# Loading the filter rows of a spectral layer: GpSimd gathers against strided loads on the SP queue

## The chip, the core and the metric

The kernel runs on one core of a Trainium2 chip. The metric is device microseconds from the start to the end of one execution. A profile of one execution shows the five engines of the core: TensorE (PE, with its weight loads shown as PEld), VectorE (DVE), ScalarE (ACT), GpSimd (POOL) and SyncE (SP). SP computes nothing here. It issues DMAs, which run on 16 DMA engines that all issuers share. The row labelled SPq, ACTq or POOLq is the issue of a DMA, not its data movement.

## What is computed

The inputs are `x` (1 x 2048 x 640), a complex filter `w_r + i w_i` (2048 x 321), and the three weights of a gated feed-forward layer (640 x 1536 twice, 1536 x 640), all in bf16.

```python
def reference(A_x, A_w_r, A_w_i, B_x, B_w_gate, B_w_up, B_w_down):
    def _A_ref(x, w_r, w_i):
        X = rfft2(x)                    # over rows and columns: 2048 x 321, complex
        X = X * (w_r + 1j * w_i)
        return irfft2(X, s=(S, D))
    def _B_ref(x, w_gate, w_up, w_down):
        return (_gelu(x @ w_gate) * (x @ w_up)) @ w_down
    x = A_x
    xn = _layernorm(x, axis=-1)
    s = _A_ref(xn, A_w_r, A_w_i)
    g = _silu(_B_ref(xn, B_w_gate, B_w_up, B_w_down))
    return x + s * g
```

So there are two branches on the same normalised `xn`: a two-dimensional Fourier filter, and a feed-forward layer with 2048 x 640 x 1536 multiply-adds three times over. They meet only in the last line.

## The kernel before

The feed-forward branch is plain matmul work: `gate_up` (L806, matmuls on L818, gelu on ACT at L830, product on DVE at L834) and `down` (L846, matmuls on L878, then tanh on ACT at L887 and DVE at L892), in four groups of 512 rows. PE fills its time with it whenever the spectral branch has nothing ready.

The spectral branch has three stages.

* **Forward, first half.** `stats`, `apply` and `fold` normalise `x` and fold it. Two matmuls (L497, L498) per slab do the first part of the row transform, and the result goes to a DRAM scratch `D2` in eight stores. The task of store `j` is called `stored[j]`. Other slabs are transposed for the feed-forward branch by DMA (`turn_dma`, L461).
* **`spectral(G)`, for G = 0 to 7.** Four DMAs (`regroup`, L533) read `D2` back into `BU` in another order. For each block G of 128 frequency pairs, PE transforms (`sp<-T,BU` on L601 and, for two of the blocks, L584), ACT or DVE copies the result out of PSUM (`Z`, `zt`), PE transforms along the row (L624, L631), and DVE multiplies by the filter: `m1` on L663 and `m3` on L671, both `mc<-WF,mb`, read the filter tile `WF`. PE then transforms back (L706), ACT or DVE copies to `IU`, and SP stores it to a scratch `D3`.
* **Inverse, second half.** Four DMAs bring `D3` back, and `inverse` (L728) runs from about 152 us on.

A frequency k and its mirror S - k are worked on together, so each block needs two sets of 128 filter rows, of `w_r` and of `w_i` each. Row numbers of a block are not contiguous: a lane's row is `8 G + c + 128 k1`, with c from 0 to 7 and k1 from 0 to 15, and its mirror is 2048 minus that. `make_tables` (L29) writes the row numbers into a table `LANE`, and `gather(G)` (L548) issues four indirect DMAs on POOL (L557), of 128 rows of 642 bytes each, into `WF[G % 3]`. There are three such tiles, so the gather for block G waits until `m3` of block G - 3 has read its tile. Before the gathers of blocks 1 and 2 stands a one-element copy on POOL (`gate`, L554), which reads `BU` and so holds these gathers back until part of `BU` has landed.

Block 0 is special: rows 0 and 1024 and the rows 64 + 128 j stand in one block, in lanes that don't follow the formula.

The order on every engine is worked out beforehand by a planner (`Plan`, L127). Each piece of work is a task with an engine, an occupation and a latency in ns, a rank, and the tasks it comes after. A DMA's landing is modelled by one shared wire (`self.wire`, L199) that is pushed back by each DMA's size. The planner's result is only an order: each engine runs its instructions in that order. What an instruction really waits for on the chip are the data it reads and the buffers it overwrites, not the planned time and not the `after` list. The gather is planned with 4200 ns on POOL; a DMA issue on SP or ACT with 430 ns.

Of the kernel before, what the change touches and what calls it, by code (L numbers as in the profile page):

```python
# [28 lines left out]
def make_tables():  # L29

    th = 2 * np.pi / D
    n2 = np.arange(128)
    n1 = np.arange(16)
    f1 = np.zeros((128, 128))
    for g in range(NG):
        for s in range(4):
            k2 = 4 * g + s
            f1[:, 8 * g + s] = np.cos(2 * np.pi * n2 * k2 / 128)
            f1[:, 8 * g + 4 + s] = -np.sin(2 * np.pi * n2 * k2 / 128)
    f1[:, 4] = np.cos(np.pi * n2)  # L40
    t2 = np.zeros((NG, 2, 4, 16, 2, 16, 4))
    ti = np.zeros((NG, 2, 16, 4, 2, 4, 16))
    for g in range(NG):
        for s in range(4):
            k2 = 4 * g + s
            for k1 in range(16):
                if k2 == 0 and k1 == 0:
                    t2[g, 0, s, :, 0, 0, s] = 1
                    t2[g, 0, s, :, 1, 0, s] = (-1.0) ** n1
                    ti[g, 0, 0, s, 0, s, :] = 1  # L50
                    ti[g, 1, 0, s, 0, s, :] = (-1.0) ** n1
                elif k2 == 0:
                    part = 0 if k1 < 8 else 1
                    ph = 2 * np.pi * n1 * (128 * k1 if k1 < 8 else 64 + 128 * (k1 - 8)) / S
                    t2[g, part, s, :, 0, k1, s] = np.cos(ph)
                    t2[g, part, s, :, 1, k1, s] = -np.sin(ph)
                    ti[g, 0, k1, s, part, s, :] = np.cos(ph)
                    ti[g, 1, k1, s, part, s, :] = -np.sin(ph)
                else:
                    ph = 2 * np.pi * n1 * (k2 + 128 * k1) / S  # L60
                    c, sn = np.cos(ph), np.sin(ph)
                    t2[g, 0, s, :, 0, k1, s] = c
                    t2[g, 1, s, :, 0, k1, s] = sn
                    t2[g, 0, s, :, 1, k1, s] = -sn
                    t2[g, 1, s, :, 1, k1, s] = c
                    ti[g, 0, k1, s, 0, s, :] = c
                    ti[g, 1, k1, s, 0, s, :] = -sn
                    ti[g, 0, k1, s, 1, s, :] = sn
                    ti[g, 1, k1, s, 1, s, :] = c
    t2 = t2.reshape(NG, 128, 128).transpose(1, 0, 2)  # L70
    ti = ti.reshape(NG, 128, 128).transpose(1, 0, 2)
    d = np.arange(160) + 0.5
    je = np.arange(0, 321, 2)
    jo = np.arange(1, 322, 2)
    ce = np.cos(th * np.outer(d, je))
    ce[:, 160] = 0
    co = np.cos(th * np.outer(d, jo))
    co[:, 160] = 0
    se = np.sin(th * np.outer(d, je))
    se[:, 0] = 0  # L80
    so = np.sin(th * np.outer(d, jo))
    so[:, 160] = 0
    fm = np.stack([ce, co, se, so, -ce, -co])[:, 0:128].transpose(1, 0, 2)
    ft = np.concatenate([ce[128:], so[128:], co[128:], se[128:]])
    ft = np.stack([ft, -ft], axis=1)
    nn = 0.5 / (S * D)
    wc = np.full(161, 2 * nn)
    wc[0] = nn
    wc[160] = 0
    ws = np.full(161, 2 * nn)  # L90
    ws[160] = nn
    ws[0] = 0
    ice, ise = (ce * wc).T, (se * ws).T
    ise[160] = np.sin(th * 320 * d) * nn
    ico, iso = (co * 2 * nn).T, (so * 2 * nn).T
    im = np.stack([ice[0:128], ico[0:128], iso[32:160], ise[33:161]]).transpose(1, 0, 2)
    it = np.concatenate([ice[128:160], ico[128:160], iso[0:32], ise[1:33]])
    lane = np.zeros((2, 16, 4, 8, 2), np.int32)
    for h in range(2):
        for k1 in range(16):  # L100
            for s in range(4):
                for G in range(8):
                    k = 8 * G + 4 * h + s + 128 * k1
                    if G == 0 and h == 0 and s == 0 and k1 >= 8:
                        k = 64 + 128 * (k1 - 8)
                    lane[h, k1, s, G] = k, (S - k) % S
    lane[0, 0, 0, 0, 1] = S // 2
    cast = lambda a: np.ascontiguousarray(a.reshape(128, -1)).astype(ml_dtypes.bfloat16)
    tabs = {k: cast(v) for k, v in dict(f1=f1, i1=f1.T, id=np.eye(128), t2=t2, ti=ti, fm=fm, ft=ft, im=im, it=it).items()}
    tabs["lane"] = lane.reshape(128, 16)  # L110
    return tabs
# [15 lines left out]
class Plan:  # L127
# [11 lines left out]
    def add(self, emit, eng, cost, rank, after=(), new=(), use=(), size=0, slow=1.0, hold=0):  # L139
        engs = eng if isinstance(eng, dict) else {eng: cost}  # L140
        t = Task(emit=emit, engs=engs, rank=rank, after=list(after), new=list(new), size=size, slow=slow, hold=hold, seq=len(self.tasks))
        for s in (*new, *use):
            s.users.append(t)
        self.tasks.append(t)
        return t
# [77 lines left out]
def kernel(  # L223
# [11 lines left out]
    nc = tc.nc  # L235
# [3 lines left out]
    consts = ctx.enter_context(tc.tile_pool(name="consts", bufs=1))  # L239
    persist = ctx.enter_context(tc.tile_pool(name="persist", bufs=1))  # L240
    work = ctx.enter_context(tc.tile_pool(name="work", bufs=2))
    dpool = ctx.enter_context(tc.tile_pool(name="dscratch", bufs=1, space=bass.MemoryType.DRAM))
# [12 lines left out]
    ident = consts.tile([P, P], BF16)  # L255
    mh = consts.tile([P, 1], FP32)
    warm = consts.tile([P, 1], FP32)
    gate = consts.tile([1, 1], BF16)
    STAT = consts.tile([P, NSLAB, 12], FP32)
    MVA = consts.tile([P, NSLAB, 2], FP32)  # L260
    NM = consts.tile([P, NSLAB, 1], FP32)
# [19 lines left out]
    add = plan.add  # L281
# [11 lines left out]
    def either(n, act=0, dve=0):  # L293
        return {"ACT": c_act(n, extra=act), "DVE": c_dve(n, 1, True, extra=dve)}
# [68 lines left out]
    t = add(blank, "DVE", (330, 400), (0, -9), new=[idle])  # L363
    t = keep_warm(6, [t])
# [4 lines left out]
    t = keep_warm(3, [t, x_in[0]], 0)  # L369
# [19 lines left out]
    turned, stored, xn_of = {}, {}, {}  # L389
# [75 lines left out]
    def fold(j, aps):  # L465
# [26 lines left out]
        for s in range(2):  # L492
# [12 lines left out]
            outs.append(add(cp, either(640), None, (1, 2 * j + s), after=[a] + outs, new=[] if s else [A], use=[pa, A] if s else [pa]))  # L505
        stored[j] = dma(lambda: D2[:, 2 * j:2 * j + 2, :], lambda: A.tile, (0, -1, j), 327680, after=outs, use=[A], slow=1.1)

    lead = ("DVE", "DVE", "ACT", "DVE")
    for n1 in range(NSLAB):
        if n1 % 2 == 0:  # L510
            xn_of[n1 // 2] = Slot("s1")
        r = stats(n1, (lead[n1] if n1 < 4 else ("ACT" if n1 % 2 else "DVE"),))
# [13 lines left out]
    sB = Slot("xb")  # L526
    B_in = {}

    def regroup(q):
        def go(e):  # L530
            if q == 0:
                sB.tile = persist.tile([P, NSLAB, D], BF16, tag="xb", name="BU")
            nc.sync.dma_start(out=sB.tile[:, 4 * q:4 * q + 4, :],  # L533
                              in_=D2[32 * q:32 * q + 32].rearrange("(g q) n d -> (q n) g d", q=8))
        B_in[q] = add(go, "SP", (430, 430), (0, -2, q), after=[stored[j] for j in range(8)] + ([B_in[q - 1]] if q else []),
# [9 lines left out]

    W_in, W_slot = {}, {}

    def gather(G):  # L548
        sw = Slot("W")

        def go(e):
            sw.tile = WF[G % 3]
            if 0 < G < 3:
                nc.gpsimd.tensor_copy(out=gate, in_=sB.tile[0:1, 8 * G - 8, 0:1])  # L554
            for pm in range(2):
                for ri, wsrc in enumerate((A_w_r, A_w_i)):
                    nc.gpsimd.indirect_dma_start(  # L557
                        out=sw.tile[:, pm, ri, 0:L], out_offset=None, in_=wsrc,
                        in_offset=bass.IndirectOffsetOnAxis(ap=LANE[:, 2 * G + pm:2 * G + pm + 1], axis=0))
        W_in[G] = add(go, "POOL", (4200, 4200), (3, G), use=[sB] if 0 < G < 3 else [], after=[stored[7]] + ([W_in[G - 1], B_in[2 * G - 2]] if 0 < G < 3 else [W_in[G - 1]] if G else []), new=[sw],  # L560
                      size=328704, slow=1.3)
        W_slot[G] = sw
    for G in range(8):
        gather(G)
    for k in ("t2", "fm", "ft"):
        load_tab(k, (0, 1, seq[0]), after=[stored[3]])
    for k in ("ti", "i1", "im", "it"):
# [5 lines left out]
    def spectral(G):  # L573
# [122 lines left out]
        for h in range(2):  # L696
# [12 lines left out]
            def cp(e, h=h, pi=pi):  # L709
                if h == 0:  # L710
# [230 lines left out]
```

## Time and profile before

| what | value |
|---|---|
| median of 14 runs | 212.48 us (211.52 to 214.19) |
| the profiled execution | 212.15 us, of which its instructions span 210.4 us |
| mean granted clock of PE | 0.99 |
| PE busy | 196.3 us of 210.4 us |
| DVE busy | 158.4 us |
| ACT busy | 109.8 us |
| POOL busy | 55.4 us |

How to read it: the span is from the first to the last instruction, and the profiled execution's own time is 1.75 us longer than its span. An engine's busy time counts its instructions, not the issuing of DMAs by SP or ACT. A row of the timeline has the start and length in us, the engine, line and operation, what it writes and reads, and in square brackets how long the engine stood idle before it and what ended that. A row of the table by stretches has, for each engine, its busy time in that stretch and the number of instructions, then the granted clock, the mean busy share of the DMA engines, and the bytes that they moved per ns. The ends of matmuls are modelled.

### The profile page before, as it was taken

Reading aid. Unit: us, or ns where it says so; the run is one execution under the profiler, and the core shown is the slowest. Engines: PE = TensorE matmul, PEld = TensorE weight load, DVE = VectorE, ACT = ScalarE, POOL = GpSimd, SP = SyncE. Lnnn points to the kernel's source line nnn. Section 1 sums busy time; section 2 is a strip of 40 time slices with the busy share of each in tenths; the row PEclk is TensorE's granted clock in tenths of the full one; section 3 lists DMA queues with packets and bytes.
Section 4 is the critical chain, followed back from the end, with each engine's and each line's share of the span. In section 5 each row is a group of like instructions: output and inputs, shape, how many; then the busy total and the mean of one; then the engine's idle time right before and its main releaser. Section 6 shows DMA issues by size and latency. Waiting matters only on the chain.

```text
span 210.4 us, 3946 instructions
## 1 busy us (share of the span) xinstructions
PE 196.3 (93%) x1463; PEld 117.0 (56%) x1479; DVE 158.4 (75%) x337; ACT 109.8 (52%) x188; POOL 55.4 (26%) x83
## 2 busy tenths in 40 slices
PE   7599999999999689997998999999999999999991
PEld 2494444567545345584764545447764555556780
DVE  3879899985323369996979899892257978999884
ACT  2579774354423367765686444424155456555521
POOL 3405241144037303552744820000000220222210
PEclk9799999999999999999999999999999999999999
DMA  5999999848597500231331350113930322333431
GB/s 139 325 319 338 359 306 225 194 130 218 200 350 243 166 3 0 63 95 36 107 99 48 109 175 0 64 62 76 350 138 5 115 62 75 119 110 94 156 117 62
DMA packets 30978, 30.78 MB, mean 146 GB/s; under 512 B 10576, under 2 KB 27488, under 8 KB 30960
## 3 DMA queue, kind: packets, MB, share of 16 engines
q1 hardware_dynamic: 27712, 24.16, 38.4%
q0 software_dynamic: 2368, 5.30, 9.7%
q10 hardware_dynamic: 880, 1.09, 1.7%
q8 instruction: 11, 0.18, 0.3%
q14 instruction: 7, 0.06, 0.1%
HBM read 20.70 MB, written 7.86 MB: 136 GB/s over the span
## 4 chain that ended last, share of the span: by engine, by line
PE 83%; DVE 8%; ACT 2%; DMA 2%; issue 2%; another core or an unknown queue 1%; SPq 1%; DVEq 0%
PE pu L818 23%; PE pg L818 22%; PE pg L878 12%; PE pu L878 11%; PE sp L706 3%; PE sp L764 3%; PE sp L631 2%; PE sp L740 2%; DMA X<-in_A_x_dram 2%; PE sp L497 2%; PE sp L601 1%; DVE uT L834 1%; PE sp L624 1%; PE sp L758 1%
## 5 line engine op out<-in xcount | busy, mean ns | idle before, releaser
L818 PE MATMUL pg<-xnT,Wg 128*128 128x512 bf16 (+1 forms) x262 | 60.0, 358 | 2.2 <-ACT xnT L291 1.2
L818 PE MATMUL pu<-xnT,Wu 128*128 128x512 bf16 (+1 forms) x262 | 60.5, 357 | 0.4
L830 ACT ACTIVATE ge<-pg 128x512 bf16<-128x512 f32 x48 | 28.5, 595 | 38.1 <-PE pg L818 28.3
L834 DVE TENSOR_TENSOR uT<-pu,ge 128x512 bf16<-128x512 f32 x48 | 33.1, 690 | 19.5 <-PE pu L818 13.6
L878 PEld LDWEIGHTS <-uT 128*128 128x128 bf16 x396 | 37.5, 98 | 12.7
L818 PEld LDWEIGHTS <-Wg 128*128 128x128 bf16 x270 | 25.0, 99 | 25.3 <-issue 2.0
L818 PEld LDWEIGHTS <-Wu 128*128 128x128 bf16 x270 | 24.7, 99 | 21.2
L291 ACT CAST ma<-sp 128x644 bf16<-128x644 f32 (+1 forms) x29 | 23.2, 801 | 17.0 <-PE sp L764 8.6
L878 PE MATMUL pg<-Wd,uT 128*128 128x320 bf16 (+2 forms) x204 | 31.8, 293 | 0.0
L878 PE MATMUL pu<-Wd,uT 128*128 128x320 bf16 (+1 forms) x192 | 31.0, 297 | 0.0
L843 POOL DMA_DIRECT2D xr<-in_A_x_dram x16 | 8.7, 549 | 73.0 <-DVE res L866 73.0
L557 POOL DMA_INDIRECT WF<-in_A_w_r_dram,LANE x16 | 16.4, 1022 | 26.5 <-DVE mc L671 23.5
L557 POOL DMA_INDIRECT WF<-in_A_w_i_dram,LANE x16 | 17.0, 1061 | 4.9 <-issue 4.9
L422 POOL TENSOR_TENSOR RSTD<-MVA,mh 128x1 f32<-128x1 f32 x16 | 9.7, 609 | 18.9 <-DVE MVA L404 18.3
L892 DVE SCALAR_TENSOR_TENSOR G<-th,pg 128x320 bf16<-128x320 f32 (+2 forms) x17 | 8.0, 468 | 7.1 <-ACT th L887 6.1
L887 ACT ACTIVATE th<-pg 128x320 f32<-128x320 f32 (+2 forms) x17 | 7.3, 427 | 11.4 <-PE pg L878 10.9
L892 DVE SCALAR_TENSOR_TENSOR G<-th,pu 128x320 bf16<-128x320 f32 (+1 forms) x16 | 7.7, 480 | 6.6 <-ACT th L887 6.5
L887 ACT ACTIVATE th<-pu 128x320 f32<-128x320 f32 (+1 forms) x16 | 7.0, 435 | 10.4 <-PE pu L878 8.1
L400 DVE BATCH_NORM_STATS2 STAT<-X 128x6 f32<-128x320 bf16 x18 | 8.3, 484 | 3.0 <-DMA X<-in_A_x_dram 3.0
L291 ACT CAST IU<-sp 128x640 bf16<-128x640 f32 x12 | 8.1, 693 | 2.8 <-PE sp L706 2.8
L291 ACT CAST Z<-sp 128x1024 bf16<-128x1024 f32 x7 | 7.0, 1019 | 4.5 <-PE sp L706 1.9
L291 ACT CAST mc<-sp 128x640 bf16<-128x640 f32 x13 | 8.4, 698 | 0.8 <-PE sp L498 0.8
(79 smaller groups left out, 236.3 us busy)
## 6 DMA issues: line engine op xcount, KB each, us to landing
BU<-D SPq DMA_DIRECT2D x8, 640.0 KB
D<-mc SPq DMA_DIRECT2D x8, 320.0 KB
D<-IU SPq DMA_DIRECT2D x8, 320.0 KB
xr<-in_A_x_dram POOLq DMA_DIRECT2D x16, 160.0 KB
out_dram<-res SPq DMA_DIRECT2D x15, 160.0 KB
Wg<-in_B_w_gate_dram SPq DMA_DIRECT2D x6, 320.0 KB
Wu<-in_B_w_up_dram SPq DMA_DIRECT2D x6, 320.0 KB
Wd<-in_B_w_down_dram SPq DMA_DIRECT2D x2, 960.0 KB
```

The source lines that it names most:

```text
L291: return nc.scalar.copy(out=out, in_=in_) if e == "ACT" else nc.vector.tensor_copy(out=out, in_=in_)
L400: nc.vector.bn_stats(out=STAT[:, n1, 6 * g:6 * g + 6], in_=x[:, 320 * g:320 * g + 320])
L422: nc.gpsimd.tensor_tensor(out=rstd, in0=var, in1=mh, op=ALU.pow)
L557: nc.gpsimd.indirect_dma_start(out=sw.tile[:, pm, ri, 0:L], out_offset=None, in_=wsrc, in_offset=bass.IndirectOffsetOnAxis(ap=LANE[:, 2 * ...
L706: nc.tensor.matmul(pt[:, pq, at:at + 2 * (hi - lo)], lhsT=TI[:, 2 * G + h, :], rhs=v[:, :, lo:hi], start=True, stop=True, skip_group_check ...
L818: nc.tensor.matmul(ps.tile[:, lo:hi], lhsT=w[:, c, t * P:(t + 1) * P], rhs=xnT[:, c, grp * 512 + lo:grp * 512 + hi], start=(c == 0), stop= ...
L830: nc.scalar.activation(out=ge.tile, in_=pg.tile, func=ACT.Gelu_apprx_tanh)
L834: nc.vector.tensor_tensor(out=u.tile, in0=pu.tile, in1=ge.tile, op=ALU.mult)
L843: nc.gpsimd.dma_start(out=sx.tile, in_=xv[:, n1, :])
L878: nc.tensor.matmul(ps.tile[:, 0:hi - lo], lhsT=uT[grp, t].tile[:, j * P:(j + 1) * P], rhs=Wd[:, t, lo:hi], start=(t == 0), stop=(t == 11))
L887: nc.scalar.activation(out=th.tile[:, 0:hi - lo], in_=ps.tile[:, 0:hi - lo], func=ACT.Tanh, scale=0.5)
L892: nc.vector.scalar_tensor_tensor(out=G2.tile[:, lo:hi], in0=th.tile[:, 0:hi - lo], scalar=1.0, in1=ps.tile[:, 0:hi - lo], op0=ALU.add, op1 ...
```

## The change

Block 0 keeps its gather on POOL. For blocks 1 to 7 `fetch(G)` takes the place of `gather(G)`:

* The order of the lanes in a block is changed from (h, k1, s) to (h, s, k1), in the tables `t2`, `ti` and `lane`. Lane 16 c + k1 then holds row `8 G + c + 128 k1`, so a plain strided DMA can load the 128 rows. One for `w_r` and one for `w_i` are issued on SP. Shapes of matmuls and tables stay as they were.
* The mirrored rows come from a new DRAM scratch `D4` of 16 x 64 x 2 x 322 elements. Two DMAs from DRAM to DRAM, issued on ACT, write it once: they read 16 x 56 rows backwards (a step of -L), one DMA for `w_r` and one for `w_i`. Each block then takes its mirrored rows of both with one strided DMA on SP.
* In the plan the two copies come after `stored[3]`, with size 575232 on the modelled wire each. The loads of a block come after `stored[7]`, after the loads of the block before, and for blocks 1 and 2 after a part of `BU`. These are constraints of the planned order; on the chip the loads wait for their `WF` tile and, for the mirrored rows, for `D4`.
* The `gate` copies go. POOL is left with the root of the variance (L422), the four gathers of block 0 and the loads of `xr` (L843).

```diff
-    t2 = np.zeros((NG, 2, 4, 16, 2, 16, 4))
-    ti = np.zeros((NG, 2, 16, 4, 2, 4, 16))
+    t2 = np.zeros((NG, 2, 4, 16, 2, 4, 16))
+    ti = np.zeros((NG, 2, 4, 16, 2, 4, 16))
...
-    lane = np.zeros((2, 16, 4, 8, 2), np.int32)
+    lane = np.zeros((2, 4, 16, 8, 2), np.int32)
...
-                    lane[h, k1, s, G] = k, (S - k) % S
+                    lane[h, s, k1, G] = k, (S - k) % S
...
-    gate = consts.tile([1, 1], BF16)
...
+    D4 = dpool.tile([NSLAB, 64, 2, LP], BF16)
...
+    turned_w = []
+    for ri, w in enumerate((A_w_r, A_w_i)):
+        turned_w.append(add(lambda e, ri=ri, w=w: nc.scalar.dma_start(
+            out=D4[:, 8:64, ri, :], in_=bass.AP(tensor=w.tensor, offset=w.offset + 120 * L, ap=[[P * L, NSLAB], [-L, 56], [1, LP]])),
+                            "ACT", (430, 430), (1, 0), after=[stored[3]], size=575232, slow=1.5))
+
+    def fetch(G):
+        sw = Slot("W")
+        W_slot[G] = sw
+
+        def go(e, ri, w):
+            sw.tile = WF[G % 3]
+            nc.sync.dma_start(out=sw.tile[:, 0, ri, 0:L], in_=w.rearrange("(k c) f -> c k f", c=P)[8 * G:8 * G + 8])
+
+        def back(e):
+            nc.sync.dma_start(out=sw.tile[:, 1].rearrange("p r f -> p (r f)"), in_=D4[::-1, 8 * G:8 * G + 8].rearrange("a c r f -> c a (r f)"))
+        hold = [stored[7], W_in[G - 1]] + ([B_in[2 * G - 2]] if G < 3 else [])
+        t = [add(lambda e, ri=ri, w=w: go(e, ri, w), "SP", (430, 430), (3, G), after=hold, new=[] if ri else [sw], use=[sw] if ri else [], size=82176, slow=1.2)
+             for ri, w in enumerate((A_w_r, A_w_i))]
+        W_in[G] = add(back, "SP", (430, 430), (3, G), after=t + turned_w, use=[sw], size=164352, slow=1.2)
+
     def gather(G):
         sw = Slot("W")
 
         def go(e):
             sw.tile = WF[G % 3]
-            if 0 < G < 3:
-                nc.gpsimd.tensor_copy(out=gate, in_=sB.tile[0:1, 8 * G - 8, 0:1])
             for pm in range(2):
...
-        W_in[G] = add(go, "POOL", (4200, 4200), (3, G), use=[sB] if 0 < G < 3 else [], after=[stored[7]] + ([W_in[G - 1], B_in[2 * G - 2]] if 0 < G < 3 else [W_in[G - 1]] if G else []), new=[sw],
+        W_in[G] = add(go, "POOL", (4200, 4200), (3, G), after=[stored[7]], new=[sw],
                       size=328704, slow=1.3)
         W_slot[G] = sw
-    for G in range(8):
-        gather(G)
+    gather(0)
+    for G in range(1, 8):
+        fetch(G)
```

More of the change, by code (lines that the diff above doesn't have):

```diff
@@ L47, in make_tables @@
                 if k2 == 0 and k1 == 0:
[L48 to L51, printed above, removed]
+                    t2[g, 0, s, :, 0, s, 0] = 1
+                    t2[g, 0, s, :, 1, s, 0] = (-1.0) ** n1
+                    ti[g, 0, s, 0, 0, s, :] = 1
+                    ti[g, 1, s, 0, 0, s, :] = (-1.0) ** n1
                 elif k2 == 0:
@@ L54, in make_tables @@
                     ph = 2 * np.pi * n1 * (128 * k1 if k1 < 8 else 64 + 128 * (k1 - 8)) / S
[L55 to L58, printed above, removed]
+                    t2[g, part, s, :, 0, s, k1] = np.cos(ph)
+                    t2[g, part, s, :, 1, s, k1] = -np.sin(ph)
+                    ti[g, 0, s, k1, part, s, :] = np.cos(ph)
+                    ti[g, 1, s, k1, part, s, :] = -np.sin(ph)
                 else:
@@ L61, in make_tables @@
                     c, sn = np.cos(ph), np.sin(ph)
[L62 to L69, printed above, removed]
+                    t2[g, 0, s, :, 0, s, k1] = c
+                    t2[g, 1, s, :, 0, s, k1] = sn
+                    t2[g, 0, s, :, 1, s, k1] = -sn
+                    t2[g, 1, s, :, 1, s, k1] = c
+                    ti[g, 0, s, k1, 0, s, :] = c
+                    ti[g, 1, s, k1, 0, s, :] = -sn
+                    ti[g, 0, s, k1, 1, s, :] = sn
+                    ti[g, 1, s, k1, 1, s, :] = c
     t2 = t2.reshape(NG, 128, 128).transpose(1, 0, 2)
```

## Prediction, written before the changed kernel was run

> **What bounds the kernel now.** First the page: its span, the busy time of the engines, and the chain that ended last.
>
> ```profile
> span 210.4 us, 3946 instructions
> ...
> PE 196.3 (93%) x1463; PEld 117.0 (56%) x1479; DVE 158.4 (75%) x337; ACT 109.8 (52%) x188; POOL 55.4 (26%) x83
> ...
> PE 83%; DVE 8%; ACT 2%; DMA 2%; issue 2%; another core or an unknown queue 1%; SPq 1%; DVEq 0%
> ```
>
> PE bounds it: 196.3 of 210.4 us, and 83% of the chain. The removed gathers stand on POOL, which is not in the chain at all. So the change can only gain where PE stands idle, 210.4 - 196.3 = 14.1 us. Where that is, the table of stretches shows (stretch, length, PE busy, PEld, DVE, ACT, POOL, clock, DMA share, GB/s).
>
> ```profile
> 0.00:10.00 10.00, 6.35 (x31) 3.23 (x32) 5.56 (x19) 4.09 (x8) 4.10 (x15) 0.90 0.80 228
> ...
> 30.00:40.00 10.00, 9.95 (x52) 4.78 (x52) 9.35 (x25) 4.93 (x9) 1.93 (x3) 1.00 1.25 202
> 40.00:50.00 10.00, 10.00 (x76) 7.06 (x74) 8.48 (x22) 4.19 (x9) 4.21 (x5) 1.00 0.63 170
> 50.00:60.00 10.00, 9.95 (x59) 5.56 (x59) 3.33 (x6) 4.33 (x9) 0.55 (x1) 1.00 0.74 230
> 60.00:70.00 10.00, 9.95 (x65) 5.28 (x65) 3.30 (x4) 2.51 (x4) 7.34 (x10) 1.00 0.91 300
> 70.00:80.00 10.00, 7.74 (x59) 3.75 (x59) 5.89 (x11) 5.60 (x8) 0.64 (x1) 1.00 0.12 32
> 80.00:90.00 10.00, 9.95 (x88) 5.87 (x88) 9.77 (x22) 7.43 (x11) 4.55 (x4) 1.00 0.14 34
> 90.00:100.00 10.00, 8.49 (x90) 6.38 (x88) 8.12 (x17) 5.80 (x10) 4.03 (x4) 1.00 0.26 68
> 100.00:110.00 10.00, 9.69 (x93) 6.87 (x91) 8.61 (x18) 7.73 (x12) 6.23 (x6) 1.00 0.32 101
> 110.00:120.00 10.00, 8.94 (x67) 4.90 (x69) 9.11 (x18) 6.33 (x10) 6.43 (x7) 1.00 0.30 86
> 120.00:130.00 10.00, 9.95 (x55) 4.88 (x55) 9.57 (x18) 4.15 (x7) 2.13 (x4) 1.00 0.32 96
> ...
> 200.00:210.40 10.40, 5.74 (x55) 4.64 (x52) 6.74 (x21) 1.92 (x5) 0.54 (x1) 0.95 0.26 87
> ```
>
> Start and tail lose 3.65 and 4.66 us, and the change touches neither. From 70 to 120 us, in the spectral stage, PE loses 2.26 + 0.05 + 1.51 + 0.31 + 1.06 = 5.19 us. That is all there is to win. The next question is what those gaps wait for; the timeline of PE, ACT, DVE and POOL answers it.
>
> ```profile
> 63.83 1.06 PE L601 MATMUL sp<-T,BU 128*128 128x128 bf16 x16
> 65.80 1.24 PE L818 MATMUL pg<-xnT,Wg 128*128 128x512 bf16 x5
> 66.49 1.01 ACT L291 CAST Z<-sp 128x1024 bf16<-128x1024 f32 x1 [1.87 <-PE pu L818]
> 70.77 0.60 ACT L830 ACTIVATE ge<-pg 128x512 bf16<-128x512 f32 x1 [3.26 <-PE pu L818]
> 72.89 1.22 DVE L291 CAST zt<-sp 128x1024 bf16<-128x1024 f32 x1
> 74.17 0.32 PE L624 MATMUL sp<-FT,zt 32*128 32x161 bf16 x8 [1.51 <-DVE zt L291]
> ...
> 75.79 0.45 PE L631 MATMUL sp<-FM,Z 128*128 128x161 bf16 x4
> 76.27 0.89 ACT L291 CAST ma<-sp 128x644 bf16<-128x644 f32 x1 [0.47 <-PE sp L631]
> ...
> 93.93 0.61 PE L601 MATMUL sp<-T,BU 128*128 128x128 bf16 x8
> 96.92 1.01 ACT L291 CAST Z<-sp 128x1024 bf16<-128x1024 f32 x1 [1.93 <-PE sp L706]
> 97.98 0.46 PE L706 MATMUL sp<-R,TI 128*128 128x256 bf16 x4 [1.51 <-ACT Z L291]
> ...
> 115.95 0.32 PE L624 MATMUL sp<-FT,zt 32*128 32x161 bf16 x7 [0.87 <-DVE IU L291]
> ```
>
> Normally a reader starts as soon as PE is done: L631 ends at 75.79 + 0.45 = 76.24, and ACT copies at 76.27. At 64.89 L601 is done, but the second copy of `Z` starts only at 66.49, 1.6 us late; `pg` is done at 67.04, but its gelu starts at 70.77, 3.7 us late; L601 is done at 94.54, its copy starts at 96.92, 2.4 us late. ACT and DVE are idle and wait for PE, which by its own rows has finished. PE runs ahead until its buffers are full, then stands idle: the 1.51 us before 74.17 and before 97.98. Now POOL and the filter tile:
>
> ```profile
> 49.61 0.95 POOL L557 DMA_INDIRECT WF<-in_A_w_i_dram,LANE  x1 [0.30 <-issue]
> 60.50 0.18 POOL L554 COPY gate<-BU 1x1 bf16<-1x1 bf16 x1 [9.95 <-DMA BU<-D]
> 60.84 0.97 POOL L557 DMA_INDIRECT WF<-in_A_w_r_dram,LANE  x1 [0.16 <-issue]
> 69.69 0.95 POOL L557 DMA_INDIRECT WF<-in_A_w_i_dram,LANE  x1 [0.30 <-issue]
> 82.23 1.29 POOL L557 DMA_INDIRECT WF<-in_A_w_r_dram,LANE  x1 [11.59 <-DVE mc L671]
> 94.81 1.20 POOL L557 DMA_INDIRECT WF<-in_A_w_i_dram,LANE  x1 [0.30 <-issue]
> 115.43 0.95 POOL L557 DMA_INDIRECT WF<-in_A_w_r_dram,LANE  x1 [2.04 <-DVE mc L671]
> 119.47 0.94 POOL L557 DMA_INDIRECT WF<-in_A_w_i_dram,LANE  x1 [0.30 <-issue]
> 120.41 1.72 POOL L843 DMA_DIRECT2D xr<-in_A_x_dram  x3
> ...
> L663 DVE TENSOR_TENSOR mc<-WF,mb x8: 820/824/830, 78.6 to 126.8; 128x1288 bf16<-128x1288 bf16 x8
> ```
>
> The late releases lie inside or just behind a run of gathers: 60.84 to 70.64, and the run that ends at 96.01. From 120.4 on, without gathers, PE loses 0.05 us in ten. I read this as: while POOL builds the descriptors of a gather, PE's completion is told late. It is not proven: the runs from 82.23 and from 115.43 are gathers too, and PE lost only 0.05 us from 80 to 90.
>
> **The change, part by part.**
>
> *The gathers of blocks 1 to 7 leave POOL.* That `WF` came late is no part of the loss: no DVE instruction has a filter DMA as its releaser, and the last gather is issued by 120.41 us, 6.4 us before the last `m1` (126.8). What goes, by my reading, is the late telling: 5.19 us at most, nothing at least.
>
> *What is late next.* DVE. It works 5.89 + 9.77 + 8.12 + 8.61 + 9.11 = 41.5 us in these 50 us. Without the loss the same work fits into about 45 us, 92%; from 120 to 130 us it stands at 96% and PE still loses only 0.05. So nearly all of the gap can close. I leave 0.9 us standing, the gap before 115.95, whose releaser is DVE at the end of a long run of its own work.
>
> *The fetches on SP.* 21 DMA issues. The nearest row, the second of these three, has four issues of a load in 2.30 us:
>
> ```profile
> 32.80 0.34 SPq L298 DMA_DIRECT2D D<-mc  x1
> 56.25 2.30 SPq L533 DMA_DIRECT2D BU<-D  x4
> 42.09 0.44 ACT L887 ACTIVATE th<-pg 128x320 f32<-128x320 f32 x1 [2.93 <-PE pg L878]
> ```
>
> That is 0.58 us each, 1.7 us a block, where POOL took 119.47 + 0.94 - 115.43 = 5.0 us. Landing: the first of the `BU` loads, twice a block's bytes, was there 60.50 - 56.25 = 4.2 us after issue; I take that as the upper end, so the last block stands in `WF` by 115.4 + 1.7 + 4.2 = 121.3 us, before 126.8. Blocks 1 and 2 queue behind all of `BU`, as the gate made them do. A fetch that waits for `m3` has the `D3` stores queued behind it on SP. Those are read only when all eight are there, and `IU` has two buffers, so a store may be late by about one block ((126.8 - 78.6) / 7 = 6.9 us). Cost: none, between zero and the 0.9 us already left.
>
> *The two copies to `D4` on ACT.* They wait for no data. Two issues at 0.58 us (between 0.4 and 3 us) come after the fourth store of `D2`, issued at 32.80; I put them, an estimate, a few us behind it, where ACT has idle time, 2.93 us before 42.09. If that cover were gone, the tanh would be 1.2 us late, and PE has finished matmuls ahead there. Their data, 2 x 16 x 56 x 644 bytes = 1.15 MB, take 3.8 us at the 300 GB/s of 60 to 70 us and 6.8 us at the 170 of 40 to 50. From 40 to 60 us the DMA engines are busy 6.3 + 7.4 us of 20, so 6.3 us are free.
>
> *Three `xr` loads move ahead.* Behind the gathers at 120.41 nothing held them back but POOL's order. Now they follow block 0's gather at 49.61 + 0.95, about 50.6 us: 0.49 MB, 1.6 us at 300 GB/s, just ahead of the `BU` loads.
>
> *Both together against `BU`.* `BU` landed by 60.50 and is first used at 63.83: 3.3 us of cover. With free DMA time used, at most 6.8 + 1.6 - 6.3 = 2.1 us of delay; with none of it, 8.4, which would cost PE 5.1. I take zero, as the row of free time is the nearest.
>
> *The lanes.* Same shapes, same number of instructions: nothing. That planned times of loads and the wire shift can swap neighbours in the order; I have no row for that, and keep it within the residual on one side and the whole gain on the other.
>
> Sum on the profiled execution: 212.15 - 5.19 + 0.9 = 207.9. The median of the runs lies 0.33 above that execution, so 208.2 us.
>
> **Rivals.**
>
> *Same: the releases are late for another reason.* For it: the two runs of gathers without loss. Against it: every loss in mid-kernel begins by a run of gathers. Then PE loses its 5.19 us as now: 212.5. The Trainium skill, page "SBUF — State Buffer", section "Who interferes with whom", says that PE and ACT never wait on anyone and that only DVE and GpSimd share ports; by that rule gathers can't hold PE's results up, and this rival holds. The 2.4 us at 96.92 speak against taking it that far, though the rule is on ports and a completion may go another way.
>
> *Slower: the lateness goes with the traffic of small rows, not with POOL.* The 28 gathers move 3584 rows and cost 5.19 us, 1.45 ns a row. The change moves 7 x 384 = 2688 rows in fetches and 1792 in copies, 4480, or 6272 if a copy's row counts for its read and its write: 6.5 to 9.1 us, that is 1.3 to 3.9 us slower, 213.8 to 216.4. It decides if PE's completions come late near the copies and the fetches too. Against it: 30 to 40 us has the busiest DMA engines of all (1.25) and PE at 9.95.
>
> *Part of the gain: `BU` late.* If the copies and `xr` loads use no free time, PE waits before L601 for up to 5.1 us; half of it leaves 210.5 to 211.8.
>
> **The numbers.** Forecast (206.3 to 210.5) 0.66; part of the gain 0.10; same 0.14; slower 0.10. 0.3% is 0.64 us, about what a measurement of this kernel can tell from no change. So faster 0.76, same 0.14, slower 0.10. The low end is the full gain and 0.7 us from DVE's earlier end; the high end takes in the same time.
>
> **What would show it.** Right: no ACT or DVE copy starts over 1 us after PE's row has ended behind 51 us; PE at 9.9 of ten from 60 to 120 us; `m1` never waits for a DMA. Wrong: gaps of 1.5 us before L624 and L706 stay with POOL empty (same); late releases at 37 to 50 us or at each fetch (slower); L601 waits for `BU` (part). A reordered plan would show as PE idle behind 120 us, or a longer tail than 4.66 us.

## The result and the profile after

The changed kernel takes 207.85 us (median of 10 executions, 206.75 to 209.22). The kernel before took 212.66 us in the same comparison (47 executions). The ratio is 0.9788, with a 95% interval from 0.9765 to 0.9811: 2.1% faster. Ratios, here and below, leave out executions over 1.5% above the fastest of their kernel, so they need not be the quotient of the medians. Forecast were 208.2 us, with 206.3 to 210.5 at a chance of 0.66. The profiled execution took 208.44 us, where the prediction's sum gave 207.9.

The page of the kernel after. All lines of code behind the new function stand 20 further down (L818 is L838, L601 is L621, L887 is L907).

```profile
span 206.6 us, 3929 instructions
...
PE 196.2 (95%) x1461; PEld 117.3 (57%) x1479; DVE 158.0 (76%) x335; ACT 111.5 (54%) x190; POOL 25.9 (13%) x53
```

PE is busy as long as before (196.2 against 196.3 us), so all of the gain is idle time of PE: 206.6 - 196.2 = 10.4 us in place of 14.1. POOL has lost 29.5 us of work; DVE and ACT work as long as before to within 2 us. The table by stretches says where the idle time went (columns as in the prediction).

```profile
0.00:10.00 10.00, 6.55 (x34) 3.15 (x35) 5.48 (x19) 4.42 (x8) 4.00 (x15) 0.96 0.79 225
...
50.00:60.00 10.00, 8.96 (x55) 5.11 (x55) 3.28 (x6) 4.63 (x9) 2.65 (x4) 1.00 1.08 254
60.00:70.00 10.00, 9.95 (x59) 5.02 (x59) 3.75 (x6) 3.12 (x5) 0.00 (x0) 1.00 0.96 318
70.00:80.00 10.00, 9.95 (x73) 4.99 (x74) 5.66 (x10) 5.17 (x8) 0.00 (x0) 1.00 0.49 128
80.00:90.00 10.00, 9.89 (x89) 6.12 (x90) 9.78 (x21) 7.21 (x10) 0.00 (x0) 1.00 0.13 33
90.00:100.00 10.00, 10.00 (x105) 7.63 (x103) 9.60 (x20) 8.53 (x14) 0.00 (x0) 1.00 0.22 68
100.00:110.00 10.00, 9.95 (x97) 6.60 (x96) 9.57 (x20) 8.13 (x12) 0.00 (x0) 1.00 0.35 109
110.00:120.00 10.00, 9.14 (x68) 5.01 (x68) 8.49 (x16) 6.56 (x10) 0.00 (x0) 1.00 0.30 89
...
200.00:206.60 6.60, 2.38 (x28) 2.03 (x26) 3.65 (x12) 1.21 (x4) 0.00 (x0) 1.00 0.20 66
```

From 70 to 120 us PE now loses 0.05 + 0.11 + 0 + 0.05 + 0.86 = 1.07 us, where it lost 5.19: a gain of 4.12. The tail loses 4.22 in place of 4.66 and the start 3.45 in place of 3.65. Against that stands one new loss: 1.04 us from 50 to 60, where it was 0.05. The sum, -4.12 - 0.44 - 0.20 + 0.99 = -3.77 us, is the change of the span (-3.8).

The timeline of the kernel after shows the new loss, the first copies of the spectral stage, and what is left at 117 us.

```profile
46.01 1.10 POOL L576 DMA_INDIRECT WF<-in_A_w_r_dram,LANE  x1 [0.18 <-issue]
...
49.09 0.98 PE L898 MATMUL pg<-Wd,uT 128*128 128x320 bf16 x6
...
50.02 0.95 POOL L576 DMA_INDIRECT WF<-in_A_w_i_dram,LANE  x1 [0.30 <-issue]
...
51.53 0.98 PE L898 MATMUL pu<-Wd,uT 128*128 128x320 bf16 x6
52.10 0.44 ACT L907 ACTIVATE th<-pg 128x320 f32<-128x320 f32 x1 [4.54 <-PE pu L898]
...
53.50 0.38 PE L497 MATMUL sp<-mb,F1T 128*128 128x512 bf16 x1 [0.99 <-ACT mc L291]
...
68.62 1.06 PE L621 MATMUL sp<-T,BU 128*128 128x128 bf16 x16
69.27 1.01 ACT L291 CAST Z<-sp 128x1024 bf16<-128x1024 f32 x1 [0.93 <-PE sp L621]
...
117.19 0.32 PE L644 MATMUL sp<-FT,zt 32*128 32x161 bf16 x7 [0.81 <-ACT IU L291]
```

`Z` is now copied while L621 is still running, as its first half is done; before, its second copy came 1.6 us behind the end. But at the four gathers that stayed, those of block 0 from 46.01 to 50.97, a tanh is late: the last six matmuls of its `pg` end at 50.07, it starts at 52.10, 2.0 us later, and ACT was idle all that time. PE runs ahead to 52.51 and then waits 0.99 us. That is the picture of before, at the one place where gathers are left. Near the gap of 0.81 us before 117.19 there is no gather.

### The profile page after: what moved, and what is told of

It is laid out like the page before. It is cut to its first block, busy times and chain, and to the rows that moved or that the text cites. A ratio compares the mean times of both kernels' runs of the same rounds, so it can differ in the third digit from the quotient of the medians.

```text
span 206.6 us, 3929 instructions
## 1 busy us (share of the span) xinstructions
PE 196.2 (95%) x1461; PEld 117.3 (57%) x1479; DVE 158.0 (76%) x335; ACT 111.5 (54%) x190; POOL 25.9 (13%) x53
## 4 chain that ended last, share of the span: by engine, by line
PE 89%; DVE 3%; ACT 2%; DMA 2%; issue 1%; SPq 1%; DVEq 0%; ACTq 0%
PE pg L838 24%; PE pu L838 24%; PE pu L898 12%; PE pg L898 12%; PE sp L651 3%; PE sp L784 3%; PE sp L726 2%; PE sp L760 2%; DMA X<-in_A_x_dram 2%; PE sp L497 2%; PE sp L621 2%; PE sp L644 1%; PE sp L778 1%; DVE G L912 1%; DVE uT L854 1%
## 5 line engine op out<-in xcount | busy, mean ns | idle before, releaser
L838 PE MATMUL pg<-xnT,Wg 128*128 128x512 bf16 (+1 forms) x262 | 60.5, 358 | 1.9 <-ACT xnT L291 1.4
L838 PE MATMUL pu<-xnT,Wu 128*128 128x512 bf16 (+1 forms) x260 | 59.9, 359 | 0.3
L838 PEld LDWEIGHTS <-Wg 128*128 128x128 bf16 x270 | 25.1, 100 | 24.4 <-issue 1.2
L838 PEld LDWEIGHTS <-Wu 128*128 128x128 bf16 x270 | 24.9, 100 | 21.2
L291 ACT CAST ma<-sp 128x644 bf16<-128x644 f32 (+1 forms) x30 | 24.0, 799 | 11.4 <-PE sp L784 6.0
L907 ACT ACTIVATE th<-pg 128x320 f32<-128x320 f32 (+2 forms) x17 | 7.2, 425 | 17.3 <-PE pg L898 12.1
L422 POOL TENSOR_TENSOR RSTD<-MVA,mh 128x1 f32<-128x1 f32 x16 | 10.3, 646 | 19.4 <-DVE MVA L404 18.8
L291 ACT CAST IU<-sp 128x640 bf16<-128x640 f32 x15 | 10.2, 690 | 2.2 <-PE sp L726 2.1
L907 ACT ACTIVATE th<-pu 128x320 f32<-128x320 f32 (+1 forms) x16 | 6.9, 434 | 8.1 <-PE pu L898 7.7
L291 ACT CAST Vt<-sp 128x640 bf16<-128x640 f32 x10 | 6.9, 690 | 3.0 <-PE sp L760 2.8
L291 ACT CAST mc<-sp 128x640 bf16<-128x640 f32 x12 | 7.7, 700 | 0.8 <-PE sp L498 0.8
L704 DVE TENSOR_TENSOR R<-Y 64x644 bf16<-64x644 bf16 x16 | 7.8, 490 | 0.4
L706 DVE TENSOR_TENSOR R<-Y 64x644 bf16<-64x644 bf16 x16 | 7.8, 487 | 0.3
```

What stands on the lines that cost most here:

```text
L291: return nc.scalar.copy(out=out, in_=in_) if e == "ACT" else nc.vector.tensor_copy(out=out, in_=in_)
L422: nc.gpsimd.tensor_tensor(out=rstd, in0=var, in1=mh, op=ALU.pow)
L704: nc.vector.tensor_tensor(out=o, in0=Yf[:, ::-3, :], in1=Yf[:, 1:3, :], op=ALU.subtract)
L706: nc.vector.tensor_tensor(out=o, in0=Y[:, 0], in1=Y[:, 1], op=ALU.add)
L838: nc.tensor.matmul(ps.tile[:, lo:hi], lhsT=w[:, c, t * P:(t + 1) * P], rhs=xnT[:, c, grp * 512 + lo:grp * 512 + hi], start=(c == 0), stop= ...
L907: nc.scalar.activation(out=th.tile[:, 0:hi - lo], in_=ps.tile[:, 0:hi - lo], func=ACT.Tanh, scale=0.5)
```

## The experiments

Twelve runs were made, on four chips of one kind, each beside the kernel before on the same chip. The record does not name the chip of the first comparison. Two theories stood at first. **Theory A**: each gather that POOL builds delays the news of PE's end, and that is the whole loss. **Theory B**: the news is late for another reason, and the change won by its other order of work (the first expectation calls this second half theory C). When the first chip showed no loss in the kernel before, a third came in, **theory D**: gathers delay PE's news only under a condition that some chips have and others lack. Each chip's runs come from one session, so a condition of the chip can't be told here from one of the session; "chip" below stands for both.

| run | chip | before there, us | this, us | ratio [95% interval] |
|---|---|---|---|---|
| e1_no_loads | 6 | 207.16 | 207.06 | 0.9988 [0.9954, 1.0023] |
| e2_fetch_on_pool | 6 | 207.16 | 206.80 | 0.9965 [0.9922, 1.0008] |
| e3_no_copies | 6 | 207.16 | 207.35 | 0.9990 [0.9954, 1.0026] |
| e4_no_gather | 6 | 207.16 | 208.66 | 1.0051 [1.0021, 1.0082] |
| b1_before | 5 | 207.53 | 206.93 | 1.0005 [0.9970, 1.0040] |
| a1_after | 5 | 207.53 | 206.67 | 0.9951 [0.9915, 0.9986] |
| x1_more_gathers | 13 | 207.90 | 208.09 | 1.0005 [0.9961, 1.0049] |
| e1_no_loads_again | 13 | 207.90 | 207.23 | 0.9982 [0.9941, 1.0022] |
| a2_after | 7 | 212.82 | 207.83 | 0.9792 [0.9703, 0.9881] |
| e1_no_loads_more | 7 | 212.82 | 207.51 | 0.9767 [0.9697, 0.9836] |
| e2_fetch_more | 7 | 212.82 | 208.25 | 0.9799 [0.9714, 0.9883] |
| x1_more_gathers_more | 7 | 212.82 | 225.82 | 1.0630 [1.0545, 1.0715] |

The table has to be read by chip. On chips 5, 6 and 13 the kernel before takes 207.2 to 207.9 us; on chip 7 it takes 212.8, as in the comparison above (212.7).

**Chip 6.** *e1* is the kernel before in its own order, without the gathers of blocks 1 to 7 and the two `gate` copies before them; all blocks then read the rows of block 0.

```diff
-            sw.tile = WF[G % 3]
+            sw.tile = WF[0]
+            if G:
+                return
```

> The kernel before, every engine's order kept, but blocks 1 to 7 issue no gather and no gate copy: all blocks read block 0's filter rows (so the filter is left out for seven blocks). Theory A (building a gather's descriptors on POOL makes PE's completions known late): the mid-kernel idle time of PE falls from 5.2 us to under 1, and the time to about 207 to 208 us, ratio 0.975 to 0.98. Theory B (late for another reason, such as instruction fetches or the kernel's order): 212 us, as before. Theory C (the order that the planner makes for the changed kernel brought the gain): 211 to 212.5 us, since the order is that of before.

*e2* is the kernel after with the 21 loads issued by POOL.

```diff
-            nc.sync.dma_start(out=sw.tile[:, 0, ri, 0:L], in_=w.rearrange("(k c) f -> c k f", c=P)[8 * G:8 * G + 8])
+            nc.gpsimd.dma_start(out=sw.tile[:, 0, ri, 0:L], in_=w.rearrange("(k c) f -> c k f", c=P)[8 * G:8 * G + 8])
...
-            nc.sync.dma_start(out=sw.tile[:, 1].rearrange("p r f -> p (r f)"), in_=D4[::-1, 8 * G:8 * G + 8].rearrange("a c r f -> c a (r f)"))
+            nc.gpsimd.dma_start(out=sw.tile[:, 1].rearrange("p r f -> p (r f)"), in_=D4[::-1, 8 * G:8 * G + 8].rearrange("a c r f -> c a (r f)"))
```

> The changed kernel with the same order on PE, DVE and ACT; the 21 strided loads of blocks 1 to 7 are issued by POOL in place of SP. If it is POOL's building of descriptors as such that delays PE's completions, late releases come back in the spectral stage: with 21 issues in place of 28 some 3 to 4 us of the gain are lost, 210.5 to 212 us. If only the indirect form does it, 207.5 to 208.5 us, as the change. If it were the traffic of rows, also as the change, since the rows are the same.

*e3* is the kernel after without the two copies to `D4`; the rows of the block itself are loaded in place of the mirrored ones, by two loads where there was one.

```diff
-        turned_w.append(add(lambda e, ri=ri, w=w: nc.scalar.dma_start(
...
+        turned_w.append(add(lambda e: None, "ACT", (430, 430), (1, 0), after=[stored[3]], size=575232, slow=1.5))
...
-            nc.sync.dma_start(out=sw.tile[:, 1].rearrange("p r f -> p (r f)"), in_=D4[::-1, 8 * G:8 * G + 8].rearrange("a c r f -> c a (r f)"))
+            for ri, w in enumerate((A_w_r, A_w_i)):
+                nc.sync.dma_start(out=sw.tile[:, 1, ri, 0:L], in_=w.rearrange("(k c) f -> c k f", c=P)[8 * G:8 * G + 8])
```

> The changed kernel with the same order, without the two DRAM to DRAM copies; the mirrored rows are read forward from the inputs by two loads per block (so the mirrored filter rows are wrong ones). The changed kernel has a new idle stretch of PE of 1 us at 50 to 60 us, behind a release that came 4 us late during block 0's gather. Theory A with an addition (a gather delays PE's completions more when other DMAs run beside it): that gap goes and the time is 206.5 to 207.2 us. If the copies cost nothing: 207.5 to 208.2, the gap stays.

*e4* is the kernel after with no gather at all: block 0 takes the rows of block 1, by three more DMAs on SP.

```diff
-                    nc.gpsimd.indirect_dma_start(
...
+                nc.sync.dma_start(out=sw.tile[:, 0, ri, 0:L], in_=w.rearrange("(k c) f -> c k f", c=P)[8:16])
+            nc.sync.dma_start(out=sw.tile[:, 1].rearrange("p r f -> p (r f)"), in_=D4[::-1, 8:16].rearrange("a c r f -> c a (r f)"))
```

> The changed kernel with the same order, and block 0's gather too is replaced by strided loads on SP (of block 1's rows, so block 0 is filtered with wrong rows); no gather is left. Theory A: the gap of 1 us at 50 to 60 us goes although the copies still run, 206.5 to 207.2 us. If the copies alone make PE's completions late: it stays, 207.5 to 208.5 us, and releases over 1 us late remain at 46 to 52 us.

Here the kernel before took 207.16 us with all of its 32 gathers, and e1, without 28 of them, the same. Theory A in its plain form, a price for each gather, is refuted. The expectations had taken the lateness for granted; in these four traces there is none to take away, so what e2, e3 and e4 asked about it stays open here. (The release "4 us late" in the expectation of e3 is ACT's idle time of 4.54 us; 2.0 us of it lie behind the end of the matmuls.) e2 and e3 can't be told from the kernel before either; so on this chip neither the copies nor the issuing engine cost anything that shows. e4 is the only one that stands apart, 0.5% slower. The profile of e4 shows a new wait, on ACT and not on POOL. (The profiled execution took 212.35 us, 3.7 us above the median, with a granted clock of 0.71 from 70 to 80 us; so the wait isn't a measure of the median's 0.5%. Its L836 and L848 are L818 and L830 of the kernel before.)

```profile
66.56 0.34 ACTq L323 DMA_DIRECT2D TI<-tab_ti  x1
...
71.75 0.33 ACTq L323 DMA_DIRECT2D I1T<-tab_i  x1
...
74.02 0.45 ACTq L323 DMA_DIRECT2D IT<-tab_it  x1
74.56 1.08 ACT L848 ACTIVATE ge<-pg 128x512 bf16<-128x512 f32 x2 [7.00 <-DMA I1T<-tab_i]
...
75.21 1.01 PE L836 MATMUL pg<-xnT,Wg 128*128 128x512 bf16 x2 [3.49 <-ACT ge L848]
```

The four table loads on ACT depend on no data, yet they are issued over 7.5 us; in the kernel after they take 69.27 to 71.73. A semaphore is a counter that one piece of work raises and another waits for; the trace has the times of its rises. They show why ACT waits: each of these issues uses for its own landing the semaphore of a load that SP issued 7 to 12 us before (`BU` or `WF`), and the last three start 0.02 to 0.12 us behind the landing of that load. The gelu behind them is late, and PE stands idle for 3.49 us. Nothing was run to confirm that this is the 0.5%.

**Chip 5.** Both kernels unchanged, to see where the lateness had gone.

> The kernel before, unchanged, to see whether its late releases of PE are there on the chip of the experiments, where the kernel before took 207.2 us in place of 212.7. Theory A as I had it (each gather always delays PE): 212 us and idle stretches of 1.5 us before L624 and L706. Theory D (the delay needs a condition that this chip, or this allocation of the program, doesn't have): 207 us, no release over 1 us late, although the gathers are the same.

> The changed kernel, unchanged, on the same chip. Theory A: 207.5 us beside 212 of the kernel before. Theory D: about 207.3, no difference from the kernel before beyond 0.3%; the change then is worth 2% where the condition holds and nothing where it doesn't.

The kernel before on chip 5, the run of eight gathers, whose loss on the prediction's chip was 1.6 and 3.7 us of lateness:

```profile
60.42 0.97 POOL L557 DMA_INDIRECT WF<-in_A_w_r_dram,LANE  x1 [0.16 <-issue]
...
63.97 1.01 ACT L291 CAST Z<-sp 128x1024 bf16<-128x1024 f32 x1 [0.30 <-PE sp L601]
...
66.13 0.60 ACT L830 ACTIVATE ge<-pg 128x512 bf16<-128x512 f32 x1 [1.15 <-PE pg L818]
...
69.27 0.94 POOL L557 DMA_INDIRECT WF<-in_A_w_i_dram,LANE  x1 [0.30 <-issue]
```

The gathers stand at the same place and are just as long (0.94 to 0.97 us, every 1.25 us), and ACT copies `Z` 0.03 us behind L601's end (its row is 62.88 and 1.06 long). In this trace PE's semaphore counts 220 of the 221 recorded ends that raise it within 0.05 us (for the other no rise is recorded), beside all 32 gathers. So the loss hangs on the chip (or the session) as well as on the program. On chip 5 the change is still worth 0.5% (0.9951); where that comes from wasn't looked into; theory D had expected at most 0.3%.

**Chip 13.** *x1* puts 16 more gathers behind those of block 7, into two tiles that nothing reads, where PE had lost nothing (the kernel is else the one before; its lines from the gather on stand about 5 further down: L823 is L818, L835 is L830, L839 is L834).

```diff
+    SPARE = [persist.tile([P, 2, 2, LP], BF16, name=f"SPARE{i}") for i in range(2)]
...
+            for i in range(16 if G == 7 else 0):
+                nc.gpsimd.indirect_dma_start(
+                    out=SPARE[i // 4 % 2][:, i // 2 % 2, i % 2, 0:L], out_offset=None, in_=(A_w_r, A_w_i)[i % 2],
+                    in_offset=bass.IndirectOffsetOnAxis(ap=LANE[:, i:i + 1], axis=0))
```

> The kernel before with 16 more gathers on POOL behind those of block 7, from about 120 to 140 us, into a spare tile that nothing reads; the order of the other engines is kept. There PE loses 0.05 us in ten without them. Theory A (each gather delays PE): 28 gathers cost 5.2 us in the first profile, so 16 cost about 3 us, wherever it runs. Theory D (the delay needs a condition that only some chips or allocations have): 3 us more than the kernel before where that kernel takes 212 us, and no difference where it takes 207 us.

> The kernel before without the gathers of blocks 1 to 7 (block 0's filter rows are used for all), again. Where the kernel before takes 212 us, theories A and D both expect 207; if it stays at 212, the gathers are not the cause of the late releases at all. Where the kernel before takes 207, no difference.

No effect of either: here gathers cost nothing, taken away or added. What was still open was whether gathers cause the loss where there is one.

**Chip 7.** The last four runs met a chip that has it: the kernel before took 212.82 us.

> The kernel after, unchanged, beside the kernel before on the chip that is given. If that chip shows late releases in the kernel before (its time about 212), the ratio is 0.976 to 0.982, as in the first comparison. If it shows none (its time 206.5 to 208), the ratio is 0.992 to 0.999, what the other chip gave (0.9951). A ratio near 0.98 at a time before of 207 would say that the gain doesn't hang on the late releases.

> The kernel before in its own order, with the gathers of blocks 1 to 7 left out. If the chip shows late releases and the gathers make them: the ratio is 0.975 to 0.985 and PE is at 9.9 from 60 to 100 us. If the chip shows late releases and something else makes them: ratio 1.00, and the late Z and ge stay. If the chip shows none: 0.996 to 1.002, as on two chips so far.

> The kernel after with its 21 strided loads issued by POOL. On a chip with late releases: if only gathers make them, the time is that of the kernel after within 0.3%; if any DMA that POOL builds makes them, ACT or DVE starts over 1 us late beside the loads, and the time is 1 to 5 us above that of the kernel after. On a chip without: within 0.3% of the kernel after.

> The kernel before with 16 more gathers between 120 and 140 us, into a tile that nothing reads. On a chip with late releases: if gathers make them wherever they stand, PE loses another 1 to 4 us there (32 gathers cost about 5 us, 0.16 us each, so 16 cost 2.6). On a chip without: no loss, within 0.5% of before, as on the first chip that ran it.

All four answer. The kernel after gives 0.9792, the first comparison again. e1, which has the order of before and lacks only gathers and the two `gate` copies, gives 0.9767: no less than the whole gain, without anything else of the change. Theory B falls. The stretches of e1 on chip 7:

```profile
60.00:70.00 10.00, 9.95 (x64) 5.26 (x64) 4.22 (x6) 3.80 (x6) 0.00 (x0) 1.00 0.97 333
70.00:80.00 10.00, 9.89 (x81) 5.43 (x82) 7.42 (x14) 6.66 (x9) 0.00 (x0) 1.00 0.01 2
80.00:90.00 10.00, 10.00 (x91) 6.15 (x89) 9.65 (x21) 6.50 (x10) 0.00 (x0) 1.00 0.01 2
90.00:100.00 10.00, 10.00 (x105) 7.35 (x104) 9.72 (x21) 7.75 (x12) 0.00 (x0) 1.00 0.18 66
```

x1 on the same chip keeps the gathers of before and has 16 more, from 120.24 on. It loses at the old places, and most of all at the new one:

```profile
60.00:70.00 10.00, 9.51 (x62) 5.01 (x61) 3.16 (x4) 2.43 (x4) 7.30 (x10) 1.00 0.92 298
70.00:80.00 10.00, 8.20 (x60) 4.02 (x61) 5.96 (x12) 5.53 (x8) 0.69 (x1) 1.00 0.13 35
80.00:90.00 10.00, 9.95 (x89) 5.81 (x88) 9.77 (x21) 7.44 (x11) 4.55 (x4) 1.00 0.15 34
90.00:100.00 10.00, 8.45 (x89) 6.33 (x88) 8.08 (x17) 5.83 (x9) 4.02 (x4) 1.00 0.26 68
...
120.00:130.00 10.00, 7.07 (x38) 3.27 (x37) 4.61 (x9) 1.98 (x3) 7.63 (x8) 1.00 0.36 97
130.00:140.00 10.00, 4.75 (x14) 1.69 (x14) 2.40 (x4) 0.60 (x1) 7.57 (x9) 0.54 0.25 60
140.00:150.00 10.00, 6.52 (x24) 2.65 (x24) 6.11 (x11) 3.60 (x6) 2.61 (x4) 0.61 0.32 99
```

On chip 13 the same kernel, with the same POOL work in the same stretches, has:

```profile
120.00:130.00 10.00, 9.95 (x55) 4.84 (x54) 9.46 (x18) 3.81 (x7) 7.57 (x8) 1.00 0.43 121
130.00:140.00 10.00, 9.95 (x64) 5.62 (x63) 7.46 (x14) 4.30 (x7) 7.00 (x9) 1.00 0.50 138
```

The timeline of x1 on chip 7 shows two of the late releases from end to end (`pg` has two buffers, used in turn, and each gelu reads the older one):

```profile
122.46 1.24 PE L823 MATMUL pg<-xnT,Wg 128*128 128x512 bf16 x5
...
124.62 1.24 PE L823 MATMUL pg<-xnT,Wg 128*128 128x512 bf16 x5
...
128.05 0.69 DVE L839 TENSOR_TENSOR uT<-pu,ge 128x512 bf16<-128x512 f32 x1 [5.31 <-remote]
...
128.79 1.24 PE L823 MATMUL pu<-xnT,Wu 128*128 128x512 bf16 x5 [2.93 <-DVE uT L839]
...
132.23 0.60 ACT L835 ACTIVATE ge<-pg 128x512 bf16<-128x512 f32 x1 [5.71 <-remote]
132.87 1.87 PE L823 MATMUL pg<-xnT,Wg 128*128 128x512 bf16 x4 [2.84 <-ACT ge L835]
...
135.14 0.69 DVE L839 TENSOR_TENSOR uT<-pu,ge 128x512 bf16<-128x512 f32 x1 [5.18 <-remote]
...
139.95 0.95 POOL L562 DMA_INDIRECT SPARE<-in_A_w_i_dram,LANE  x1 [0.30 <-issue]
...
142.83 0.60 ACT L835 ACTIVATE ge<-pg 128x512 bf16<-128x512 f32 x1 [10.01 <-remote]
```

The `pg` of 122.46 ends at 123.70, and its gelu starts at 132.23, 8.5 us later; PE waits for that one to write the next `pg`. The `pg` of 124.62 ends at 125.86, and its gelu starts at 142.83, 17.0 us later and 1.9 us behind the end of the last gather. "remote" says that the semaphore rose at a time when the profile saw nothing end that raises it.

The rises themselves settle what was late. PE counts its ends on one semaphore, ACT and DVE on one each. In this trace PE's count for the end at 123.70 rises at 132.20, and that for the end at 125.86 at 142.81; the two gelus start 0.03 and 0.02 us behind. DVE's product at 128.05 was released by PE's count too: its `pu` had ended at 122.62, the count rose at 127.96. (The ends are modelled, but PE had begun the groups of 124.62 and 128.79 before the count for 123.70 came.) From 110 to 146 us every recorded rise of DVE's and ACT's own counts lies within 0.02 us of an end of theirs; PE, waiting for DVE's product, starts at 128.79, 0.05 us behind its end. In the profile of before it is the same: the ends at 64.88 and 67.04 are counted at 66.47 and 70.75. So it is PE's count that comes late, and neither the reader nor DVE holds the gelu up.

I had expected 2.6 us of loss for the 16 gathers and no more than 4; the median rose by 225.82 - 212.82 = 13.0. The profiled execution, the longest of four, has 201.0 us of PE's work in a span of 226.4. Against the first profile of before that is 16.0 us more: 11.3 of idle PE, and 4.7 of longer matmuls, since the granted clock was 0.54 and 0.61 in the two stretches where PE had stood idle.

e2 on chip 7 has POOL build 21 plain DMAs in the place of 28 gathers, and takes what the kernel after takes (208.25 against 207.83 us). Its stretch from 90 to 100 us:

```profile
90.00:100.00 10.00, 10.00 (x106) 7.67 (x105) 9.60 (x21) 8.21 (x14) 3.54 (x6) 1.00 0.30 79
```

In 90 to 100 us POOL is busy almost as long as in x1 (3.54 and 4.02), with plain loads here and gathers there, and PE loses nothing here and 1.55 there. So it isn't any DMA from POOL that does it, but gathers; whether that is their indirect form, or that one keeps POOL for 0.95 us and more where a plain load takes 0.6, e2 doesn't tell. (The stretch from 50 to 60 us, with the late tanh behind block 0's gathers, has PE at 9.04 in e2 and 9.06 in the kernel after on chip 7; it has 9.95 in e2 on chip 6 and in the kernel after on chip 5.)

Theory D stands: on some chips, or in some sessions, runs of gathers on POOL make PE's results known late. What such a chip has, the runs don't tell. Nor do they tell why one run of gathers, 82.30 to 87.76 us, costs nothing on chip 7 either (9.95). What the table shows is that DVE was busy 9.77 there, and 2.40 to 8.08 in the four full stretches of gathers with loss; whether that is the reason wasn't tried.

## Why the prediction was right

- **PE bounds, and only its idle time can be won.** So it was: PE's busy time is the same to 0.1 us, and the gain equals the idle time that went.
- **The reading that gathers make PE's completions late.** Right for the chip of the profile, and shown by e1 on chip 7: without them, and with nothing else changed but the `gate` copies, the time falls by 2.3%, about 5 us. The semaphore rises show it directly, in the profile of before too. What the step lacked is the condition. On chips 5, 6 and 13 no price of the same gathers shows, the kernel before takes 207.2 to 207.9 us, and the change is worth 0.5% on the one of them where it was run (chip 5). The two runs of gathers without loss, which the prediction named as its doubt, were a sign of a condition; why they cost nothing is still unexplained.
- **The gain of 5.19 - 0.9.** It measured 4.12 us, against 4.29. The 0.9 left standing is still there, 0.86 from 110 to 120 us, about as long in e1 on chip 7 (9.20 of 10, without a gather there); but it ends with ACT's copy of `IU`, not with DVE. The sign that PE would be at 9.9 from 60 to 120 us so fails in this one stretch (9.14), where the sum itself had left 0.9.
- **The profiled execution lies 0.5 us above the sum**, and the term that was left out is block 0's gathers: they stay, and the stretch behind them loses 1.04 us. Before, it lost 0.05. These rows of the timeline of before show that the lateness was there already:

```profile
48.68 0.98 PE L878 MATMUL pg<-Wd,uT 128*128 128x320 bf16 x6
49.49 0.98 PE L878 MATMUL pu<-Wd,uT 128*128 128x320 bf16 x6
...
49.91 0.44 ACT L887 ACTIVATE th<-pg 128x320 f32<-128x320 f32 x1 [1.59 <-PE pg L878]
...
51.40 0.44 ACT L887 ACTIVATE th<-pu 128x320 f32<-128x320 f32 x1 [1.04 <-PE sp L498]
```

  The two tanh were 0.25 and 0.9 us late, and PE had other work meanwhile; after, it is 2.0 us, and PE runs out of work. The prediction named late releases at 37 to 50 us as a sign for the *slower* rival, copies that delay PE. One came, but on chips 5 and 6 the copies run in the same place and nothing is late. Whether on a chip like 7 their traffic makes the lateness of these gathers longer wasn't tried there by itself: e1, without copies, has a tanh 1.0 us late and PE at 9.95 from 50 to 60 us on chip 7, the kernel after 1.9 us and 9.06, but its order differs too. A better start and tail (0.64 us) gave most of the loss back. The prediction had said that the change touches neither, so that part of the hit is luck.
- **The range.** Its low end is 212.15 - 5.19 - 0.7 = 206.3, without the 0.33 between execution and median that the forecast has; with it, 206.6. The forecast's band ends at 210.5; the "high end" that takes in the 212.5 of *same* would be that of a wider range, which the text doesn't give. Neither matters for 207.85.
- **DVE next.** From 80 to 110 us DVE stands at 96% or more and PE still loses only 0.16 us. Right.
- **Fetches on SP.** The groups of their rows in the kernel after (minimum, median, maximum in ns; first and last start), and of `m1`:

```profile
L560 SPq DMA_DIRECT2D WF<-in_A_w_r_dram x7: 596/629/1059, 62.5 to 113.5; - x7
...
L563 SPq DMA_DIRECT2D WF<-D x7: 582/582/636, 64.0 to 114.8; - x7
...
L683 DVE TENSOR_TENSOR mc<-WF,mb x8: 820/823/830, 79.9 to 126.2; 128x1288 bf16<-128x1288 bf16 x8
```

  An issue costs 0.6 us, as estimated at 0.58. The last is issued at 114.8 and its `m1` starts at 126.2; no `m1` waits for a DMA. The cost is none, as said.
- **The copies.** ACT issued them at 38.98 and 39.67, in the idle time before its tanh, whose wait was 2.93 us as before. e3, without copies, isn't faster than the kernel before on chip 6 (0.9990), where e2, with them, isn't slower (0.9965). So no cost shows there; the kernel after itself was not run on that chip.
- **`BU`.** Its loads were issued 3.7 us later than before (59.91 against 56.25), more than the 2.1 us of delay that I had reckoned with for their landing. They cost nothing, but not for my reason: the 3.3 us of cover would not have held it. The plan had moved L621 back, from 63.83 to 68.62, with other matmuls in its place. Such a move was in the residual; it had no term.
- **The rival *same*** falls by e1 on chip 7. The Trainium skill, page "SBUF — State Buffer", section "Who interferes with whom", says that PE and ACT never wait on anyone; taken as far as the prediction took it, it would give 1.00 there, and 0.9767 was measured. The page's rule is on ports, and what came late was a semaphore's count, so the runs don't speak against it as a rule on ports. On chips 5, 6 and 13 no such wait was seen. **The rival *slower*** falls by the fetches from 80 to 110 us, beside which PE loses 0.16 us.

## What to carry to other kernels

Where a reader of PSUM starts microseconds after PE's row has ended, look at what POOL does in that time, and try the kernel with the gathers left out before anything is rebuilt. Compare on more than one chip: the same edit was worth 2.1% in two comparisons and 0.5% in a third, on another chip, and a trace of one chip can't tell. Rows with a constant step don't need a gather, and a strided load on an idle queue was no dearer where it was run, but the profile of e4 suggests that more DMAs on one queue may hold up an issue on another.

## What the runs showed of the hardware

- One kernel, unchanged, takes 207.2 to 207.9 us on chips 5, 6 and 13 and 212.8 on chip 7, each measured in one session. In the first profile (212.15 us) the granted clock is 1.00 in the stretches from 70 to 120 us where PE loses 5.19. On chip 7 the difference goes when 28 gathers go (0.9767).
- On chip 7, beside 20 gathers in a row, PE's semaphore counted an end 17.0 us late (125.86, counted at 142.81); ACT's and DVE's rises there lie within 0.02 us of their ends. The 16 gathers added cost 13.0 us, 0.8 us each, a slower clock included, where 28 had cost about 5, 0.2 each. On chip 13 the same 16 cost nothing (1.0005).
- PE that stood idle came back at a lower clock: 0.54 and 0.61 in ten microseconds, with groups of five matmuls of 128x512 taking 2.33 us in place of 1.24.
